# Crossbar for k, half-array scores and a new order of PSUM banks in an attention kernel with an MLP behind it

## Chip, cores, metric

One core of one Trainium2 chip. The metric is device microseconds of one execution. Each median is of executions on one chip. The experiments were run in four sets on four chips (names beginning with a, b, c, d); within a set the kernels took turns with the kernel before, whose medians were 342.99, 342.67, 342.5 and 342.35 us. Medians of different sets are thus of different chips, and differences of well under 1 us between them mean little. A run over 1.5% above the fastest of its kernel counts as slow and is left out of the ratios. Ratios are the mean time of one kernel's fast runs over that of the other's of the same rounds, so they are not quite the ratio of the medians quoted beside them.

## The reference

```python
# q, k, v: [8 batches, 8 heads, 576, 64]; x: [4608, 512]
# down: q, k, v averaged over groups of 4 rows, softmax attention over 144 rows, each result row repeated 4 times
# local: softmax attention over 576 rows, masked to |i - j| < 4
x = (out_up + out_local), heads side by side
h = x @ w_in                        # 512 -> 2048
out = gelu(h) @ w_out               # 2048 -> 512
```

## The kernel before

Names used below: PE is TensorE, DVE is VectorE, ACT is ScalarE, POOL is GpSimd, SP is the engine whose queue issues DMAs. A "crossbar" transpose is a transpose done by a DMA on its way. A transfer "lands" when its data are there. PSUM is the memory that TensorE writes, in banks; a "tag" names a buffer in it that is used over and over.

Activations stay on chip in fp16. A loop runs over nine chunks of 512 tokens. In chunk c the first product "m1" (64 matmuls of 512 columns, each four followed by a gelu on ACT) has the preparation of batch c+1 between its matmuls, and the second product "m2" (64 more) has the attention of that batch between them. `fill(n)` issues the next n of them. The parts that matter:

```python
def t_in(b, p):                     # k of one pair of heads: TensorE transposes it
    nat = nat6(ld[b % 2]["kn"])
    tr = ppool.tile([128, 1024], F16, tag="tr", name="tr_k")
    for c in range(NCK):            # 6
        nc.tensor.transpose(tr[:, CH * c:CH * c + CH], nat[:, c, 2 * p:2 * p + 2, :], I128[0:CH, 0:CH])
    for hh in range(2):             # zero-padded copy for each head
        r = slice(64 * hh, 64 * hh + 64)
        nc.vector.tensor_copy(out=kz[r, p, hh, :], in_=tr[r, 0:S])
    k_sums(p)
...
def attn(b, fill, n0, n1, n2):      # n0, n1, n2 = 6, 9, 9
    fill(n0)
    if b == 1: v_down_pe(b)         # TensorE sums v of batch 1 in groups of four
    scores(b, 0)
    fill(n1)
    mask(0)
    s_lo(b)                         # scores of the last 16 averaged keys, PSUM tag "tr"
    for p in range(NP):             # 4 pairs of heads
        if p + 1 < NP: scores(b, p + 1)
        else: fill(4)
        av(b, p)                    # value products, PSUM tag "av", then DVE normalises
        if p + 1 < NP: mask(p + 1)
        if p == 2 and b + 1 < B:
            for i in range(NP): regroup("qn", i)     # DVE
            cross(b + 1)                             # crossbar transpose of q, issued on SP
        fill(n2 if p + 1 < NP else n2 + 4)
        t_out(b, p)                 # output transposes, PSUM tag "tr"; ACT copies xd, DVE adds xT
...
# chunk c, b = c + 1 from 2 on: loads and preparation beside m1
load6(b + 1, "qn")                  # GpSimd issues all loads
v_down(b)                           # GpSimd sums v
for p in range(NP):
    q_sums(b, p)                    # GpSimd sums q; waits for q's crossbar
    f1(4 if p == 0 else 14)
    t_in(b, p)
k_lo()
run(load_nat(b + 1)); run(load_v(b + 1))
f1()
```

The softmax here doesn't subtract the row's maximum and nothing guards it: scores larger than these inputs give would overflow.

## Time and profile before

| | before |
|---|---|
| median (lowest to highest) | 342.38 us (342.2 to 342.77, 4 runs) |
| span of the profiled run | 341.7 us, clock 1.0 |
| PE busy | 97% |
| one batch, m2 start to m2 start | 35.19 us |
| of the 50 us before m2 of chunk 0, PE idle | about 8 us (41.99 of 49.76 busy) |

The lines behind this table stand in the prediction, but for the last. To read a group of lines in order of time: the first number is the start, the second the length, and PE instructions overlap in their pipeline, so the distance of starts is the cost and not the length.

### The profile page before, as it was taken

How to read it: one execution, taken by the hardware profiler on the slowest of the kernel's cores; microseconds unless marked ns; L12 is line 12 of the kernel's file. 1: busy time of each engine (PE TensorE's matmuls, PEld its weight loads, DVE VectorE, ACT ScalarE, POOL GpSimd, SP SyncE). 2: the span in 40 equal slices, each digit the busy share in tenths (PEclk: the TensorE clock that was granted, in tenths of full speed). 3: DMA queues.
4: the chain of work that ended last, by engine and by line, in shares of the span. 5: the costliest groups of instructions: out<-in, count | busy, mean ns of one | idle time of the engine just before them, and what ended most of it. 6: DMA issues, size and time to landing. Idle time of an engine off the chain costs nothing.

```text
span 341.7 us, 6605 instructions
## 1 busy us (share of the span) xinstructions
PE 330.5 (97%) x2729; PEld 185.7 (54%) x2729; DVE 176.3 (52%) x316; ACT 201.2 (59%) x369; POOL 157.0 (46%) x212
## 2 busy tenths in 40 slices
PE   8698899999999999999999999999999999999995
PEld 4574446654665456555654575457555664444444
DVE  7755954857375737663766466736764650000000
ACT  8675666646764677367736764675467656514610
POOL 8973259545926890659165916697150000000000
PEclk9999999999999999999999999999999999999999
DMA  6999999993999499849985995699610010011012
GB/s 88 153 194 205 203 86 136 185 154 75 95 177 154 68 136 131 111 91 101 173 89 118 109 169 78 126 95 152 98 65 3 31 63 31 2 61 62 2 46 77
DMA packets 109198, 35.82 MB, mean 105 GB/s; under 512 B 85744, under 2 KB 104688, under 8 KB 109168
## 3 DMA queue, kind: packets, MB, share of 16 engines
q0 software_dynamic: 89824, 22.42, 72.6%
q1 hardware_dynamic: 14304, 3.80, 8.7%
q10 hardware_dynamic: 5040, 9.18, 7.8%
q8 instruction: 21, 0.34, 0.4%
q14 instruction: 9, 0.07, 0.1%
HBM read 44.83 MB, written 9.44 MB: 159 GB/s over the span
## 4 chain that ended last, share of the span: by engine, by line
PE 89%; DVE 4%; DMA 3%; POOL 1%; ACT 1%; issue 0%; DVEq 0%; ACTq 0%
PE m_ps L260 35%; PE m_ps L236 34%; PE sc L382 5%; PE av L442 3%; DMA q_nat<-in_q_dram 3%; PE tr_o L484 2%; PE tr_k L273 2%; DVE kdz L282 1%; PE av L434 1%; PE av L436 1%; PE sc L388 1%; PE m_ps L251 1%; DVE kz L306 1%; DVE nall L452 1%; POOL k_nat L139 1%; DVE nall L457 1%
## 5 line engine op out<-in xcount | busy, mean ns | idle before, releaser
L236 PE MATMUL m_ps<-xT,w_in_sb 128*128 128x512 f16 x568 | 129.5, 379 | 2.5 <-ACT gT L239 2.1
L260 PE MATMUL m_ps<-w_out_sb,gT 128*128 128x512 f16 x560 | 130.4, 379 | 0.0
L239 ACT ACTIVATE gT<-m_ps 128x512 f16<-128x512 f32 x142 | 84.3, 597 | 43.8 <-PE m_ps L236 43.5
L236 PEld LDWEIGHTS <-w_in_sb 128*128 128x128 f16 x568 | 53.7, 97 | 63.1 <-issue 3.7
L260 PEld LDWEIGHTS <-gT 128*128 128x128 f16 x560 | 51.9, 98 | 54.7
L264 ACT COPY out_sb<-m_ps 128x512 f32<-128x512 f32 x35 | 20.6, 589 | 41.2 <-PE m_ps L260 41.2
L282 DVE TENSOR_REDUCE kdz<-kz 128x288 f16<-128x1152 f16 x28 | 37.9, 1352 | 2.0 <-ACT kz L306 1.1
L289 POOL TENSOR_TENSOR q_t<-qT 128x288 f32<-128x288 f16 x28 | 20.5, 733 | 38.5 <-DMA qT<-q_nat 31.0
L420 DVE TENSOR_TENSOR e<-e,band 128x1152 f16<-128x1152 f16 x28 | 21.5, 767 | 28.0 <-ACT e L414 28.0
L277 DVE COPY kz<-tr_k 64x576 f16<-64x576 f16 x48 | 21.8, 455 | 25.5 <-PE tr_k L273 25.1
L487 DVE TENSOR_TENSOR xT<-tr_o,xd 128x576 f16<-128x576 f16 x28 | 21.2, 756 | 23.5 <-ACT xd L486 23.5
L457 DVE TENSOR_TENSOR nall<-av,rr 128x896 f16<-128x896 f32 x29 | 31.7, 1091 | 1.0
L255 DVE COPY out_sa<-m_ps 128x256 f32<-128x256 f32 x2 | 0.8, 424 | 55.1 <-PE m_ps L251 55.1
L112 POOL DMA_DIRECT2D k_nat<-in_k_dram x36 | 27.8, 779 | 0.0
L124 POOL DMA_DIRECT2D v_win<-in_v_dram x30 | 26.6, 921 | 0.3 <-issue 0.3
L139 POOL DMA_DIRECT2D q_nat<-in_q_dram x10 | 7.9, 790 | 40.1 <-DVE q_nat L146 40.1
L382 PE MATMUL sc<-qT,kz 128*128 128x120 f16 (+1 forms) x310 | 24.6, 217 | 0.0
L412 ACT ACTIVATE e<-sc 128x684 f16<-128x684 f32 x31 | 22.8, 736 | 0.0
L382 PEld LDWEIGHTS <-kz 128*128 128x128 f16 x320 | 21.4, 97 | 1.4 <-ACT kz L306 0.2
L486 ACT COPY xd<-tr_o 128x144 f16<-128x144 f16 x28 | 7.7, 274 | 24.5 <-PE tr_o L484 21.2
L414 ACT ACTIVATE e<-sc 128x468 f16<-128x468 f32 x31 | 17.6, 567 | 0.8 <-PE sc L382 0.7
L410 ACT ACTIVATE ed<-sc 128x288 f16<-128x288 f32 x31 | 12.6, 407 | 5.8 <-PE sc L382 5.7
(176 smaller groups left out, 385.4 us busy)
## 6 DMA issues: line engine op xcount, KB each, us to landing
out_dram<-out_sb ACTq DMA_DIRECT2D x35, 256.0 KB, 4.8
v_win<-in_v_dram POOLq DMA_DIRECT2D x40, 128.0 KB, 8.1
q_nat<-in_q_dram POOLq DMA_DIRECT2D x7, 576.0 KB, 11.4
k_nat<-in_k_dram POOLq DMA_DIRECT2D x36, 96.0 KB, 4.0
v_grp<-in_v_dram POOLq DMA_DIRECT2D x6, 512.0 KB, 7.9
w_in_sb<-in_moe_w_in_dram POOLq DMA_DIRECT2D x4, 512.0 KB, 9.9
w_out_sb<-in_moe_w_out_dram POOLq DMA_DIRECT2D x4, 512.0 KB, 19.8
k_nat<-in_k_dram POOLq DMA_DIRECT2D x1, 576.0 KB, 9.1
```

Source lines behind the costliest of these rows:

```text
L112: nc.gpsimd.dma_start(out=nat6(ld[b % 2]["kn"])[:, c, :, :], in_=k[b, :, CH * c:CH * c + CH, :].rearrange("h s d -> s h d"))
L124: nc.gpsimd.dma_start(out=L["vw"][:, j, :, 0:64], in_=v[b, :, W0[j]:W0[j] + 128, :].rearrange("h s d -> s h d"))
L236: nc.tensor.matmul(out=ps, lhsT=w_in_sb[:, fc, 128 * j:128 * j + 128], rhs=xT[:, fc, 512 * c:512 * c + 512], start=(fc == 0), stop=(fc == 3))
L239: nc.scalar.activation(out=g[:, j, :], in_=ps, func=ACTF.Gelu)
L260: nc.tensor.matmul(out=ps, lhsT=g[:, j, 128 * t:128 * t + 128], rhs=w_out_sb[:, j, :], start=(j == 0), stop=(j == NJ - 1))
L277: nc.vector.tensor_copy(out=kz[r, p, hh, :], in_=tr[r, 0:S])
L282: nc.vector.tensor_reduce(out=kdz[:, p, :, :], in_=kz[:, p, :, :].rearrange("p a (g r) -> p a g r", r=4), axis=AX.X, op=ALU.add)
L382: nc.tensor.matmul(out=dst, lhsT=kz[:, p, hh, W0[j]:W0[j] + 128], rhs=q6(b)[:, :, p, Q0[j] // 6:(Q0[j] + QW[j]) // 6], start=(b > 0), stop ...
L412: nc.scalar.activation(out=e2[:, :, 0:EA], in_=sc2[:, :, 0:EA], func=ACTF.Exp, scale=0.125)
L420: nc.vector.tensor_tensor(out=e2, in0=e2, in1=band.unsqueeze(1).broadcast_to([128, 2, S]), op=ALU.mult)
L457: nc.vector.tensor_tensor(out=nall.rearrange("p j a c -> p a j c"), in0=av4[:, :, :, 0:64], in1=rr.unsqueeze(3).broadcast_to([128, 2, 7, 6 ...
L487: nc.vector.tensor_tensor(out=xT[:, p, S * b:S * b + S].rearrange("p (g r) -> p g r", r=4), in0=tr[:, 0:S].rearrange("p (g r) -> p g r", r=4),
```

## The change

The intent is to take work from TensorE: k of batches 3 to 7 is transposed by DMA through the crossbar, and a pair of heads has its scores computed on the two halves of the array, by turns, so k needs no zero padding. The two halves write different banks, so scores take four banks. The separate bank "tr" is gone; output transposes and low-key scores move into "av". Loads and sums are put in another order, and so is batch 0 (a list of words, left out).

```diff
+    def cross_k(b):
+        nc.sync.dma_start_transpose(out=kP.rearrange("p c a t -> p (c a) t"), in_=ld[b % 2]["kn"])
...
+    def k_in(p):
+        nc.vector.tensor_copy(out=kT[:, p, :].rearrange("p (c t) -> p c t", c=NCK), in_=kP[:, :, p, :])
+        k_sums(p)
...
+        if b:
+            for j in (None, 0, 1, 2, 3, 4):
+                half(0, j)          # rows 0 to 63
+                half(1, j)          # rows 64 to 127
...
     def t_out(b, p):
-        tr = ppool.tile([128, 1024], F16, tag="tr", name="tr_o")
+        tr = ppool.tile([128, 1024], F32, tag="av", name="tr_o")[:, 0:512].bitcast(F16)
...                                  # attn
-            else:
+            if p:
                 fill(4)
...
-            fill(n2 if p + 1 < NP else n2 + 4)
+            fill(8 if p + 1 < NP else 12)
...                                  # chunk, b from 2 on
                 load6(b + 1, "qn")
-            v_down(b)
+                if b > 2: run(load_nat(b + 1))
+            if b == 2: v_down(b)
             for p in range(NP):
                 q_sums(b, p)
-                f1(4 if p == 0 else 14)
-                t_in(b, p)
-            k_lo()
+                if b == 2: f1(...); t_in(b, p)
+                else: k_in(p)
+            k_lo(b)
+            if b > 2: v_down(b)
+            elif b + 1 < B: run(load_nat(b + 1))
             if b + 1 < B:
-                run(load_nat(b + 1))
+                cross_k(b + 1)
                 run(load_v(b + 1))
```

More of the change, by code (lines that the diff above doesn't have):

```diff
@@ L50 @@
     ppool = ctx.enter_context(tc.tile_pool(name="ps", bufs=1, space=bass.MemoryType.PSUM))
+    early = ExitStack()
+    spool = [early.enter_context(tc.tile_pool(name="ps0", bufs=1, space=bass.MemoryType.PSUM))]
     ctx.enter_context(tc.manual_schedule())
@@ L65 @@
     band = cpool.tile([128, S], F16, tag="band", name="band")
+    kP = cpool.tile([128, NCK, NP, CH], F16, tag="kP", name="k_turned")
     turn6 = cpool.tile([128, 3, 120], F16, tag="turn6", name="turn6")
     qd = cpool.tile([128, NP, Sd], F16, tag="qd", name="qd")
+    kT = cpool.tile([128, NP, S], F16, tag="kT", name="kT")
+    kdT = cpool.tile([128, NP, Sd], F16, tag="kdT", name="kdT")
     kz = cpool.tile([128, NP, 2, S], F16, tag="kz", name="kz")
@@ L223, in m1 @@
         if c == 0:
-            half = [mm(), mm()]
-            for fcs in ((0, 1, 2), (3,)):
-                for j in range(2):
+            part = [mm(), mm(), spool[0].tile([128, 512], F32, tag="tr", name="m_ps")]
+            for fcs in ((0, 3), (1,), (2,)):
+                for j in range(3):
                     for fc in fcs:
-                        nc.tensor.matmul(out=half[j], lhsT=w_in_sb[:, fc, 128 * j:128 * j + 128],
-                                         rhs=xT[:, fc, 0:512], start=(fc == 0), stop=(fc == 3))
-                        if fc == 3:
-                            nc.scalar.activation(out=g[:, j, :], in_=half[j], func=ACTF.Gelu)
+                        nc.tensor.matmul(out=part[j], lhsT=w_in_sb[:, fc, 128 * j:128 * j + 128],
+                                         rhs=xT[:, fc, 0:512], start=(fc == 0), stop=(fc == 2))
+                        if fc == 2:
+                            nc.scalar.activation(out=g[:, j, :], in_=part[j], func=ACTF.Gelu)
                         yield
-        for j in range(2 if c == 0 else 0, NJ):
+        for j in range(3 if c == 0 else 0, NJ):
             ps = mm()
@@ L262, in m2 @@
                 if j == NJ - 1:
-                    osb = wpool.tile([128, 512], F32, tag="osb", bufs=5, name="out_sb")
+                    osb = wpool.tile([128, 512], F32, tag="osb", bufs=4, name="out_sb")
                     nc.scalar.copy(out=osb, in_=ps)
@@ L270, in t_in @@
         nat = nat6(ld[b % 2]["kn"])
-        tr = ppool.tile([128, 1024], F16, tag="tr", name="tr_k")
+        if p % 2:
+            trf = ppool.tile([128, 1024], F32, tag="av", name="tr_k")
+        else:
+            trf = spool[0].tile([128, 2048], F32, tag="sc", name="tr_k")
+        tr = trf[:, 0:512].bitcast(F16)
         for c in range(NCK):
@@ L274, in t_in @@
                                 I128[0:CH, 0:CH])
-        for hh in range(2):
-            r = slice(64 * hh, 64 * hh + 64)
-            nc.vector.tensor_copy(out=kz[r, p, hh, :], in_=tr[r, 0:S])
+        nc.vector.tensor_copy(out=kT[:, p, :], in_=tr[:, 0:S])
+        k_sums(p)
+    def k_in(p):
+        nc.vector.tensor_copy(out=kT[:, p, :].rearrange("p (c t) -> p c t", c=NCK), in_=kP[:, :, p, :])
         k_sums(p)
@@ L281, in k_sums @@
         with nc.allow_low_precision(reason="sums of four, kept in fp16 as before"):
-            nc.vector.tensor_reduce(out=kdz[:, p, :, :], in_=kz[:, p, :, :].rearrange("p a (g r) -> p a g r", r=4),
+            nc.vector.tensor_reduce(out=kdT[:, p, :], in_=kT[:, p, :].rearrange("p (g r) -> p g r", r=4),
                                     axis=AX.X, op=ALU.add)
@@ L313, in q_from, with v_down_mm @@
         cp(out=q6(b)[:, :, p, :], in_=tr.rearrange("p (r t) -> p r t", r=6))
-    def v_down_mm(L, va):
-        for j in range(5):
+    def v_down_mm(L, va, js=range(5)):
+        for j in js:
             n = 112 if j < 4 else 128
@@ L319, in v_down_mm @@
                              start=(j == 0), stop=(j == 4))
-        nc.tensor.matmul(out=va[1], lhsT=GL.rearrange("p a c -> p (a c)"), rhs=L["vw"][:, 4, :, 0:64],
-                         start=True, stop=True)
+            if j == 4:
+                nc.tensor.matmul(out=va[1], lhsT=GL.rearrange("p a c -> p (a c)"), rhs=L["vw"][:, 4, :, 0:64],
+                                 start=True, stop=True)
     def v_down_d(L, va, cp):
@@ L336, in v_down_pe, with k_lo @@
         v_down_m(L, va)
-    def k_lo():
+    def k_lo(b):
         KLb = KL.rearrange("p (a c) -> p a c", c=160)
@@ L341, in k_lo @@
             r = slice(64 * hh, 64 * hh + 64)
-            nc.vector.tensor_copy(out=KLb[r, :, 16 * hh:16 * hh + 16], in_=kdz[r, :, hh, 128:Sd])
+            nc.vector.tensor_copy(out=KLb[r, :, 16 * hh:16 * hh + 16], in_=kdT[r, :, 128:Sd] if b else kdz[r, :, hh, 128:Sd])
     def v_down(b):
@@ L358, in s_lo @@
     def s_lo(b):
-        s_lo_mm(ppool.tile([128, 512], F32, tag="tr", name="sl"))
+        s_lo_mm(ppool.tile([128, 1024], F32, tag="av", name="sl"))
         s_lo_exp(b)
@@ L374, in scores @@
     def scores(b, p):
-        sc = ppool.tile([128, 1536], F32, tag="sc", name="sc")
-        scores_mm(b, p, sc[:, 0:1024], sc[:, 1024:1536])
+        sc = spool[0].tile([128, 2048], F32, tag="sc", name="sc")
+        scores_mm(b, p, sc[:, 0:1024], sc[:, 1024:2048])
         for i in range(3):
@@ L380, in scores_mm, with q_win, padded, half @@
     def scores_mm(b, p, sA, sC):
-        def local(dst, hh, j):
-            nc.tensor.matmul(out=dst, lhsT=kz[:, p, hh, W0[j]:W0[j] + 128],
-                             rhs=q6(b)[:, :, p, Q0[j] // 6:(Q0[j] + QW[j]) // 6], start=(b > 0),
-                             stop=(b > 0 or j in (2, 4)))
-        for hh in range(2):
+        def q_win(r, j):
+            return q6(b)[r, :, p, Q0[j] // 6:(Q0[j] + QW[j]) // 6]
+        def padded(dst, hh, j):
+            nc.tensor.matmul(out=dst, lhsT=kz[:, p, hh, W0[j]:W0[j] + 128], rhs=q_win(slice(0, 128), j),
+                             start=False, stop=(j in (2, 4)))
+        def half(hh, j):
+            r = slice(64 * hh, 64 * hh + 64)
+            o = 512 * hh
+            if j is None:
+                nc.tensor.matmul(out=sA[:, o + EA:o + EA + Sd], lhsT=kdT[r, p, 0:128], rhs=qd[r, p, :],
+                                 start=True, stop=True)
+                return
+            dst = sA if j < 3 else sC
+            o += Q0[j] - (0 if j < 3 else EA)
+            nc.tensor.matmul(out=dst[:, o:o + QW[j]], lhsT=kT[r, p, W0[j]:W0[j] + 128], rhs=q_win(r, j),
+                             start=True, stop=True)
+        if b:
+            for j in (None, 0, 1, 2, 3, 4):
+                half(0, j)
+                half(1, j)
+        for hh in range(0 if b else 2):
             o = 512 * hh
@@ L389, in scores_mm @@
                              start=True, stop=True)
-            if b == 0:
-                nc.tensor.matmul(out=sA[:, o:o + EA], lhsT=I128, rhs=nb[:, 0:EA], start=True, stop=False)
+            nc.tensor.matmul(out=sA[:, o:o + EA], lhsT=I128, rhs=nb[:, 0:EA], start=True, stop=False)
             for j in range(3):
-                local(sA[:, o + Q0[j]:o + Q0[j] + QW[j]], hh, j)
-        for hh in range(2):
+                padded(sA[:, o + Q0[j]:o + Q0[j] + QW[j]], hh, j)
+        for hh in range(0 if b else 2):
             o = EC * hh - EA
-            if b == 0:
-                nc.tensor.matmul(out=sC[:, o + EA:o + S], lhsT=I128, rhs=nb[:, EA:S], start=True, stop=False)
+            nc.tensor.matmul(out=sC[:, o + EA:o + S], lhsT=I128, rhs=nb[:, EA:S], start=True, stop=False)
             for j in range(3, 5):
-                local(sC[:, o + Q0[j]:o + Q0[j] + QW[j]], hh, j)
+                padded(sC[:, o + Q0[j]:o + Q0[j] + QW[j]], hh, j)
         e = e_t[p % 3] if b else e_t0[p]
@@ L414, in exps @@
             nc.scalar.activation(out=e2[:, :, EA:S],
-                                 in_=sC[:, 0:2 * EC].rearrange("p (a c) -> p a c", c=EC),
+                                 in_=(sC.rearrange("p (a c) -> p a c", c=512)[:, :, 0:EC] if sC.shape[1] > 512
+                                      else sC[:, 0:2 * EC].rearrange("p (a c) -> p a c", c=EC)),
                                  func=ACTF.Exp, scale=0.125)
@@ L497, in to_exp, with attn @@
         nc.scalar.activation(out=dum[:, 1:2], in_=dum[:, 0:1], func=ACTF.Exp)
-    def attn(b, fill, n0, n1, n2):
+    def attn(b, fill, n0, n1):
         fill(n0)
@@ L533, in spin @@
     def spin(n):
-        ps = ppool.tile([128, 512], F32, tag="tr", name="spin")
+        ps = spool[0].tile([128, 512], F32, tag="tr", name="spin")
         for _ in range(n):
@@ L540 @@
     PLAN0 = """
-        BAND Rk0:D Rq0:D Tk0:mm0 Rk1:D Tq0:mm1 KZ10:A NB Rq1:D Tk1:av QD0:A KD10:D QT0:A KZ11:D KD00:A
-        spin1 Tq1:mm1 KZ00:A KD01:D QD1:A Rk3:D spin1 S0:sc KZ01:A Rk2:D QT1:D KD11:A Rq2:D Tk2:mm0 E20
-        Rq3:D KD12:A Tq3:av KD02:A KZ12:A Tq2:mm1 QD3:D QT3:D KZ02:A QD2:D E00 QT2:D spin2 S1:av+mm0 E10
-        Tk3:mm1 E11 S2:sc KD13:D E01 KZ13:D E21 KD03:D E22 spin1 VD:av KL E02 KZ03:D E12 SL:mm0 VLM
-        VDe:A S3:sc EL AV0:av E23 AV2:mm0+mm1 E13 NA0 E03 gelu spin3 AV1:sc NA2 TO0:av XT0:A NA1 spin2
-        AV3:mm0+mm1 TO2:av NA3 XT2:A TO1:sc XT1:A spin3 TO3:av M1A:mm0+mm1 XT3:A M1B
+        BAND Rk0:D Rq0:D Tk0:mm0 Rk1:D Tq0:mm1 KD10:A NB KD00:A Tk1:av KZ10:A QT0:D KZ00:A KZ11:D QD0:D
+        KD01:A Rq1:D KD11:A spin5 S0:sc KZ01:D Tq1:mm0 Rk3:D E00 Rk2:D E10 Tk3:mm1 QD1:D QT1:D Tk2:av
+        E20 KZ13:D S1:sc KD02:A KD12:A Rq3:D KZ12:A KZ03:D Tq3:mm0 E01 Rq2:D E21 QT3:D E11 QD3:D KD13:D
+        spin4 Tq2:mm0 KD03:D KZ02:A S3:sc QD2:D KL QT2:A VD0:av E23 SL:mm1 VD1 E03 VD2 E13 VD3 VD4 S2:sc
+        VDe:A VLM EL AV0:av E22 AV3:mm0+mm1 E02 NA0 E12 spin3 AV1:sc gelu NA3 TO0:av XT0:A NA1 spin2
+        TO3:mm0+mm1 AV2:av XT3:A NA2 TO1:sc M1X:mm0+mm1+tr XT1:D TO2:av M1Y XT2:A M1B
     """
@@ L561, in banks @@
         if sl == "sc":
-            t = ppool.tile([128, 1536], F32, tag="sc", name="sc")
+            t = spool[0].tile([128, 1536], F32, tag="sc", name="sc")
             return [t[:, 0:512], t[:, 512:1024], t[:, 1024:1536]], t[:, 0:1024]
@@ L591 @@
         elif nm[:2] == "M1":
-            f1_0(6 if nm == "M1A" else 2)
+            f1_0(6 if nm == "M1X" else 3)
         elif nm[0] == "R":
@@ L605 @@
         elif nm == "KL":
-            k_lo()
+            k_lo(0)
         elif nm == "SL":
@@ L610 @@
             s_lo_exp(0)
-        elif nm == "VD":
-            slot["VD"] = banks(arg)[0]
-            v_down_mm(L0, slot["VD"])
+        elif nm[:2] == "VD" and nm != "VDe":
+            if p == 0:
+                slot["VD"] = banks(arg)[0]
+            v_down_mm(L0, slot["VD"], (p,))
         elif nm == "VDe":
@@ L631 @@
         elif nm[:2] == "XT":
-            cp(out=xT[:, p, 0:S], in_=slot["o", p][1][:, 0:S])
+            half, two = slot["o", p]
+            if two is not None:
+                cp(out=xT[:, p, 0:S], in_=two[:, 0:S])
+            else:
+                cp(out=xT[:, p, 0:512], in_=half[0])
+                cp(out=xT[:, p, 512:S], in_=half[1][:, 0:S - 512])
     load6(1, "kn")
@@ L645, in home @@
             def home(i):
-                tag, n = (("tr", 512), ("av", 1024), ("sc", 1536))[i % 3]
-                return ppool.tile([128, n], F32, tag=tag, name=f"t_{tag}")[:, 0:512]
+                tag, n = (("av", 1024), ("sc", 1536), ("tr", 512))[i % 3]
+                return (ppool if tag == "av" else spool[0]).tile([128, n], F32, tag=tag, name=f"t_{tag}")[:, 0:512]
             regroup("kn", 0)
@@ L653 @@
                 tr, _ = t_reg("kn", p, home(p), False)
-                kz_from(p, 0, tr, nc.vector.tensor_copy)
-                kz_from(p, 1, tr, nc.scalar.copy)
+                nc.vector.tensor_copy(out=kT[:, p, :].rearrange("p (t r) -> p t r", r=6),
+                                      in_=tr.rearrange("p (r t) -> p t r", r=6))
                 if p + 2 < NP:
@@ L665 @@
                 if p == 0:
-                    k_lo()
-                f1(5)
+                    k_lo(b)
+                f1(4)
             load6(2, "qn")
@@ L673 @@
                 load6(b + 1, "qn")
-            v_down(b)
+                if b > 2:
+                    run(load_nat(b + 1))
+            if b == 2:
+                v_down(b)
             for p in range(NP):
                 q_sums(b, p)
-                f1(4 if p == 0 else 14)
-                t_in(b, p)
-            k_lo()
+                if b == 2:
+                    f1(4 if p == 0 else 14)
+                    t_in(b, p)
+                else:
+                    k_in(p)
+            k_lo(b)
+            if b > 2:
+                v_down(b)
+            elif b + 1 < B:
+                run(load_nat(b + 1))
             if b + 1 < B:
-                run(load_nat(b + 1))
+                cross_k(b + 1)
                 run(load_v(b + 1))
         f1()
+        if c == 0:
+            early.close()
+            spool[0] = ctx.enter_context(tc.tile_pool(name="ps1", bufs=1, space=bass.MemoryType.PSUM))
         f2 = filler(m2(c))
@@ L686 @@
             to_exp()
-            attn(b, f2, 6, 9, 8 if b == 1 else 9)
+            attn(b, f2, 6, 9)
         f2()
```

## The prediction

> **What bounds the kernel now.** I read the page first (busy shares, the chain that ended last), then the table by stretches, then the order of time within one batch. The page says TensorE:
>
> ```profile
> PE 330.5 (97%) x2729; PEld 185.7 (54%) x2729; DVE 176.3 (52%) x316; ACT 201.2 (59%) x369; POOL 157.0 (46%) x212
> PE 89%; DVE 4%; DMA 3%; POOL 1%; ACT 1%; issue 0%; DVEq 0%; ACTq 0%
> ```
>
> The kernel loops over nine chunks of 512 tokens. In chunk c, "m1" is 64 matmuls of 512 columns (L236) with the next batch's preparation between them, "m2" is 64 more (L260) with that batch's attention between them. Starts of L236 in the chain that ended last, one per chunk, show a period of 141.98 - 106.79 = 35.19 us:
>
> ```profile
> 106.79 0.86 PE m_ps L236 x4
> 107.91 3.02 PE m_ps L236 x14
> 111.19 3.02 PE m_ps L236 x14
> ...
> 141.98 0.86 PE m_ps L236 x4
> ```
>
> A block of 14 takes 3.02 us (0.216 each), yet the next starts 3.28 us later: the six transposes of k between them cost 0.26 us. The rest of a batch, from the order of time on PE around 97 us (start, duration), is read from start to start:
>
> ```profile
> 97.10 0.20 PE L480 MATMUL tr_o<-Iw,nall 66*128 66x66 f16 x1
> ...
> 97.46 0.23 PE L388 MATMUL sc<-qd,kdz 128*128 128x144 f16 x1
> ...
> 98.12 0.19 PE L434 MATMUL av<-v_d,ed 128*128 128x65 f16 x1
> ...
> 98.66 2.11 PE L260 MATMUL m_ps<-w_out_sb,gT 128*128 128x512 f16 x9
> ```
>
> So the output transposes take 0.36 us, the twelve scores 0.66 (55 ns each), the value products 0.54. A batch's work is 128 x 0.2157 + 4 x (0.26 + 0.66 + 0.54 + 0.35) + 0.25 for the low keys = 35.1 of the 35.19: a batch has almost no waiting on PE. Waiting is only before 50 us. There 19.0 us hold 16.48 of PE, then it is full:
>
> ```profile
> 31.00:50.00 19.00, 16.48 (x113) 8.40 (x112) 12.59 (x20) 11.37 (x21) 6.61 (x10) 1.00 1.34 164
> 50.00:71.60 21.60, 21.60 (x223) 13.33 (x222) 12.81 (x21) 13.04 (x26) 16.77 (x21) 1.00 1.62 157
> ```
>
> The columns are stretch, length, busy PE, PEld, DVE, ACT, POOL, clock, DMA share, GB/s. Work removed from PE shortens a batch only as far as nothing else starts to bind.
>
> **What the Trainium skill says.** (1) "TensorEngine Tiling (Array Packing)", section Key Properties: different tiles can load and multiply in parallel, but changing the tiling mode drains TensorE. Nothing here runs in a half-array mode, so the trace before can neither confirm it nor size the drain. (2) Same page, Gotcha 1: row tiles must write different PSUM banks. That is why scores now take four banks and the former "tr" bank is gone. (3) "TensorE: Matmul & The Clock Gate", Part 3, The mechanism: weights load beside running matmuls of another row group. The 65-column products already run at 0.31 us for ten with their weight loads, so weights are not a bound at 31 ns. (4) "DMA: Bandwidth & Descriptors", Issuing engines are not separate DMA queues: all queues share the 16 DMA engines. The trace agrees in part: q's crossbar transpose took 6.2 us to land where no q load ran beside it (242.8 us), 9.2 to 14.2 elsewhere.
>
> **The change part by part.**
>
> Transposes of k. Batches 3 to 7 lose four groups: 5 x 4 x 0.26 = **-5.2 us** on PE. In exchange SP issues one more crossbar transpose per batch, with some 30 us of slack before its reader, and DVE does a copy from SBUF and a sum over half as many elements (the sum takes 1.35 us now). None of that is on the path.
>
> Scores. Six pairs in place of twelve singles: 6 x 55 ns = 0.33 us if a pair runs in the time of one, plus a drain on entry and on return. The trace gives a ceiling for a drain: a 65-column product is shown 194 ns long at a pitch of 31, so some 0.16 us of pipeline. I choose 0.1 each, an estimate: 0.53 against 0.66, so 28 x 0.13 = **-3.6 us** for batches 1 to 7.
>
> Start. The new order of batch 0 puts exponentials of pair 0 before the late loads of pairs 2 and 3, replaces spins by nine m1 products, and batch 1 needs no zero-padded halves: DVE's copy of 0.75 serves both heads, ACT's 0.63 copy goes and the sum halves. m1 of chunk 0 then no longer waits (19.0 - 16.5 = 2.5 us); I expect m2 of chunk 0 some 4 to 5 us before its 49.8. But PE then needs v of batch 1 for its group sums:
>
> ```profile
> 37.47 1.02 POOL L155 DMA_DIRECT2D v_win<-in_v_dram  x1 [1.17 <-DMA w_out_sb<-in_moe_w_out_dram]
> 51.05 1.26 PE L318 MATMUL va<-v_win,Gb 112*128 112x512 f16 x5
> ```
>
> That last load took 12.4 us to land, at 49.9; DMA is saturated until then and the change moves no bytes out. The sums now end at 52.38; they can end at 50.4 at best: **-2.0 us**, however well the start is packed.
>
> The lost "tr" bank. The output transposes and the low-key scores now live in "av". So the value products of pair p+1 cannot start before DVE has added xT of pair p. This is where I expect the gain to go. DVE around pair 2:
>
> ```profile
> 99.12 0.24 DVE L456 RECIPROCAL rr<-av 128x14 f32<-128x14 f32 x1
> 99.39 1.09 DVE L457 TENSOR_TENSOR nall<-av,rr 128x896 f16<-128x896 f32 x1
> 100.40 0.75 DVE L420 TENSOR_TENSOR e<-e,band 128x1152 f16<-128x1152 f16 x1
> 101.06 1.16 DVE L146 COPY q_nat<-q_nat 96x768 f16<-96x768 f16 x4
> 102.14 0.75 DVE L487 TENSOR_TENSOR xT<-tr_o,xd 128x576 f16<-128x576 f16 x1
> ```
>
> In program order the four regroupings of q stand before xT of pair 2. From the reciprocal to the end of xT is 3.77 us; with 0.2 from the end of the products to the reciprocal and 0.06 for the release that is 4.03. PE has between the products of pairs 2 and 3 eight m2 products, the output transposes and four more: 1.73 + 0.35 + 0.86 = 2.94. So PE waits 1.1 us, in batches 1 to 6 (batch 7 regroups nothing): **+6.6 us**. Between pairs 0, 1 and 2 there is no regrouping: products end, then 2.07 to the end of the transposes, 0.2 + 0.28 + 0.03 + 0.76 + 0.06 for xd and xT = 3.40, against 2.94 + 0.53 of scores on PE = 3.47: just hidden. Faster scores would only turn into a wait there.
>
> The end of a batch. m2's products between are now 63 of 64 before the last transposes' end, against 59. From 105.54 (end of transposes) xT of pair 3 needs until 106.81, 1.27 us. PE has one m2 product and three of m1 that don't need pair 3: 0.86. It waits 0.45 us in seven batches: **+3.2 us**. Low keys in "av": the first products wait for their exponential, about 0.05 x 7 = **+0.35 us**.
>
> Sum: -5.2 - 3.6 - 2.0 + 6.6 + 3.2 + 0.35 = -0.65, so 341.7 us.
>
> **The rivals.**
>
> Rival 1: the new waits stay hidden, and PE's saving is the time: 342.3 - 5.2 - 3.6 - 2.0 = 331.5. For it: the m2 products were redistributed (four more before the products of pairs 1 and 2), plainly to cover the bank. Against it: at pair 3 the four were there before, and the regrouping still stands ahead of xT. Half of this, or drains near zero, gives about 336.
>
> Rival 2: the drain is the whole 0.16, the scores gain nothing: 345. For: the skill's page names a drain, twice per pair of heads, 56 times. Against: only the ceiling is in the trace.
>
> Rival 3: DMA. GpSimd's sums of v move behind those of q, which wait for q's crossbar. From m1's start I have: landing at 5 to 6.2, q sums 4.8, v sums 5.4, done at 16.4; the value products need them at 18.8. Some 2.4 us of slack; k's loads now run beside the crossbar, and if it lands 4 us later PE loses 1.6 us in five batches: 350. Against: the loads follow one another in one queue, and q's own load is already beside it. Also, PE waiting from 46 to 50 us for v could lower its clock for a while; the clock row shows no such dip now.
>
> **Range and chances.** I give the sum 65 in 100, the faster half-way (336) 25 and the slower side (346) 10: 0.65 x 341.7 + 0.25 x 336 + 0.10 x 346 = 340.7 us. The range that holds 8 in 10 is 335 to 345. Two per cent is 6.85 us: faster needs under 335.5, which takes both waits mostly hidden: 0.18. Slower needs over 349.2, DMA lateness in every batch: 0.03. Within: 0.79.
>
> **What would show it.** Right: L236 blocks without gaps in chunks 2 to 6; scores of a pair at 0.45 to 0.6 us from first to next instruction; PE idle about 1.1 us before the first value product of pair 3, released by DVE's xT, in batches 1 to 6 and not in 7; 0.45 us before the fourth product of each m1; the sums of v of batch 1 waiting for v_win. PE's busy share should fall below 97% while the time hardly moves. Wrong: no idle at pair 3 (then 331 to 336), scores at 0.65 or more (345), or value products of pair 0 waiting for v_d or v_lm of GpSimd (over 346).

## The result, and the profile after

The changed kernel takes **352.88 us** (350.65 to 354.83, 4 runs) against 342.38; the ratio is 1.0303, with a 95% interval of 1.0233 to 1.0373. It is slower by 3%, outside the predicted range. A second set of two runs gave 350.78 and 353.14.

The page of the profiled run (350.65 us, span 348.9) shows what "less work" means here. PE's busy time fell by 3.3 us while the span grew by 7.2:

```profile
PE 327.2 (94%) x2610; PEld 171.7 (49%) x2610; DVE 145.5 (42%) x292; ACT 198.7 (57%) x364; POOL 156.5 (45%) x212
PEclk9999989999999998999999999999999999999999
...
PE 69%; DMA 8%; POOL 8%; DVE 7%; issue 6%; ACT 1%; POOLq 0%
```

PE's share of the chain that ended last fell from 89% to 69%; DMA rose from 3% to 8%, GpSimd ("POOL") from 1% to 8%. The clock row (40 slices of 8.72 us) has two dips that the kernel before has not, at 44 to 52 and 131 to 140 us. The starts of m1 and m2, read from the order of time on PE, say where. "Again" is the second profile of the changed kernel (span 349.1).

| us | before | after | again |
|---|---|---|---|
| m1 of chunk 0 starts | 30.55 | 26.59 | 27.03 |
| m2 of chunk 0 starts | 49.76 | 43.65 | 44.09 |
| m1 of chunk 1 starts | 71.43 | 71.18 | 73.11 |
| m2 chunk 1 to m2 chunk 2 | 35.19 | 35.21 | 35.21 |
| m2 chunk 2 to m2 chunk 3 (attention of batch 3) | 35.20 | **42.09** | **40.23** |
| m2 chunk 3 to m2 chunk 4 | 35.19 | 35.22 | 35.23 |
| m2 of chunk 7 to the end | 45.2 | 44.8 | 44.9 |

The 6 us that the new start wins are gone again before chunk 1. All steady batches are as long as before to 0.1 us. One batch is 5 to 7 us longer. The waits of PE after, longest in total first (engine and line, what ended the wait, us in total, times, longest):

```profile
PE av L470 <- DVE xT L523: 5.8, 7, 0.9
PE av L470 <- POOL v_d L367: 3.3, 1, 3.3
PE va L335 <- DMA v_win<-in_v_dram: 2.9, 4, 1.1
PE m_ps L247 <- DVE xT L523: 2.1, 7, 0.3
PE av L472 <- POOL v_lm L371: 1.7, 1, 1.7
```

The first and fourth are the two waits that the prediction worked out: 0.92 us before the value products of pair 3 in six batches (the seventh entry is short), 0.29 in the fourth product of m1 in seven. Both in order of time in one batch (lines between left out):

```profile
179.08 1.03 PE L271 MATMUL m_ps<-w_out_sb,gT 128*128 128x512 f16 x4
181.02 0.19 PE L470 MATMUL av<-v_d,ed 128*128 128x65 f16 x1 [0.92 <-DVE xT L523]
...
184.73 0.81 PE L247 MATMUL m_ps<-xT,w_in_sb 128*128 128x512 f16 x3
185.84 1.46 PE L247 MATMUL m_ps<-xT,w_in_sb 128*128 128x512 f16 x6 [0.29 <-DVE xT L523]
```

The idle time in brackets begins when the pipeline is empty. What a wait costs is again read from start to start. Four products at 0.2157 us lead from 179.08 to 179.94, and the next instruction starts at 181.02: the wait costs 1.08 us. Three lead from 184.73 to 185.38, and the fourth starts at 185.84: 0.46 us.

The second and fifth waits are batch 3. In order of time on PE, then on GpSimd:

```profile
125.89 0.24 PE L411 MATMUL sc<-qd,kdT 64*128 64x144 f16 x2
125.96 0.43 PE L416 MATMUL sc<-qT,kT 64*128 64x120 f16 x10
129.66 0.19 PE L470 MATMUL av<-v_d,ed 128*128 128x65 f16 x1 [3.27 <-POOL v_d L367]
131.57 0.21 PE L472 MATMUL av<-v_lm,eL 128*128 128x65 f16 x1 [1.72 <-POOL v_lm L371]
```

```profile
120.87 0.73 POOL L306 TENSOR_TENSOR q_t<-qT 128x288 f32<-128x288 f16 x1 [11.55 <-DMA qT<-q_nat]
...
128.35 1.27 POOL L367 TENSOR_TENSOR v_d<-v_t 128x512 f16<-128x512 f32 x1
```

GpSimd waited 11.55 us for q's crossbar, then summed q, then v, and the value products were waiting for v. The two waits are 5.0 of the 6.9 us. Another 1.2 are the eight m2 products behind them: they took 2.94 us from start to start (132.48 to 135.42) where 1.73 is usual, at a granted clock of 0.63 from 132 to 136 us. The crossbar transposes on SP's queue, start and time to issue, show what q's was behind:

```profile
91.32 6.70 SPq L162 DMA_TRANSPOSE k_turned<-k_nat  x1
103.14 7.73 SPq L159 DMA_TRANSPOSE qT<-q_nat  x1
125.23 2.93 SPq L162 DMA_TRANSPOSE k_turned<-k_nat  x1
145.22 3.58 SPq L159 DMA_TRANSPOSE qT<-q_nat  x1
```

The DMA view of the stretches around the first two gives the time from issue to landing:

```profile
k_turned<-k_nat SPq DMA_TRANSPOSE x1, 15.0
...
qT<-q_nat SPq DMA_TRANSPOSE x1, 17.7
```

k of batch 3 is the only one whose load was left behind the sums of q (those of batch 2), so its crossbar is issued among v's loads and needs 15.0 us, until 106.3. q's is issued at 103.1 and needs 17.7. In the later batches k's crossbar runs before v's loads and takes 4.8 to 4.9 us, and q's of batch 4 takes 11.3.

The start: PE on its group sums of v of batch 1, and the table by stretches (columns as in the prediction) after:

```profile
47.12 0.38 PE L335 MATMUL va<-v_win,Gb 112*128 112x512 f16 x1 [0.57 <-DMA v_win<-in_v_dram]
48.06 0.38 PE L335 MATMUL va<-v_win,Gb 112*128 112x512 f16 x1 [0.56 <-DMA v_win<-in_v_dram]
49.54 0.55 PE L335 MATMUL va<-v_win,Gb 128*128 128x512 f16 x1 [1.10 <-DMA v_win<-in_v_dram]
...
51.16 3.02 PE L271 MATMUL m_ps<-w_out_sb,gT 128*128 128x512 f16 x9
```

```profile
44.00:48.00 4.00, 2.25 (x9) 0.60 (x7) 0.00 (x0) 1.93 (x3) 3.92 (x6) 1.00 2.07 132
48.00:52.00 4.00, 2.84 (x18) 1.02 (x18) 0.69 (x1) 1.27 (x3) 3.52 (x6) 0.70 1.66 181
```

PE came early and waited for the loads as predicted. Then the granted clock fell to 0.70 of full, and the nine m2 products, shown 2.10 us long at full clock, took 3.02.

### The profile page after: what moved, and what is told of

It reads as the page before. It is cut to its first block, busy times and chain, and to the rows that moved or that the text cites. A ratio compares the mean times of both kernels' runs of the same rounds, so it can differ in the third digit from the quotient of the medians.

```text
span 348.9 us, 6372 instructions
## 1 busy us (share of the span) xinstructions
PE 327.2 (94%) x2610; PEld 171.7 (49%) x2610; DVE 145.5 (42%) x292; ACT 198.7 (57%) x364; POOL 156.5 (45%) x212
## 4 chain that ended last, share of the span: by engine, by line
PE 69%; DMA 8%; POOL 8%; DVE 7%; issue 6%; ACT 1%; POOLq 0%
PE m_ps L271 29%; PE m_ps L247 27%; DMA w_out_sb<-in_moe_w_out_dram 5%; DMA v_win<-in_v_dram 4%; DVE xT L523 3%; PE av L478 3%; PE sc L416 2%; DVE q_nat L154 2%; PE tr_o L520 2%; PE av L470 2%; POOL v_win L166 1%; PE sc L411 1%; DVE e L456 1%; PE av L472 1%; PE m_ps L262 1%
## 5 line engine op out<-in xcount | busy, mean ns | idle before, releaser
L271 PE MATMUL m_ps<-w_out_sb,gT 128*128 128x512 f16 x560 | 135.0, 384 | 0.0
L247 PE MATMUL m_ps<-xT,w_in_sb 128*128 128x512 f16 x564 | 126.4, 379 | 2.3 <-DVE xT L523 2.1
L493 DVE TENSOR_TENSOR nall<-av,rr 128x896 f16<-128x896 f32 x30 | 32.7, 1091 | 1.0
L447 ACT ACTIVATE e<-sc 128x684 f16<-128x684 f32 x32 | 23.5, 735 | 0.0
L299 DVE TENSOR_REDUCE kdT<-kT 128x144 f16<-128x576 f16 x28 | 21.0, 750 | 0.8
L492 DVE RECIPROCAL rr<-av 128x14 f32<-128x14 f32 x30 | 7.4, 246 | 30.9 <-PE av L478 30.9
L470 PE MATMUL av<-v_d,ed 128*128 128x65 f16 x120 | 11.6, 195 | 9.2 <-DVE xT L523 5.8
L472 PEld LDWEIGHTS <-eL 128*128 128x128 f16 x128 | 9.1, 98 | 13.0 <-issue 11.3
```

Source lines behind the costliest of these rows:

```text
L247: nc.tensor.matmul(out=ps, lhsT=w_in_sb[:, fc, 128 * j:128 * j + 128], rhs=xT[:, fc, 512 * c:512 * c + 512], start=(fc == 0), stop=(fc == 3))
L271: nc.tensor.matmul(out=ps, lhsT=g[:, j, 128 * t:128 * t + 128], rhs=w_out_sb[:, j, :], start=(j == 0), stop=(j == NJ - 1))
L299: nc.vector.tensor_reduce(out=kdT[:, p, :], in_=kT[:, p, :].rearrange("p (g r) -> p g r", r=4), axis=AX.X, op=ALU.add)
L447: nc.scalar.activation(out=e2[:, :, 0:EA], in_=sc2[:, :, 0:EA], func=ACTF.Exp, scale=0.125)
L493: nc.vector.tensor_tensor(out=nall.rearrange("p j a c -> p a j c"), in0=av4[:, :, :, 0:64], in1=rr.unsqueeze(3).broadcast_to([128, 2, 7, 6 ...
```

## The experiments

There were fifteen runs. Theory A: batch 3 is long because v's sums stand behind a late q crossbar. Theory D: q's crossbar is late because k's, started beside v's loads, is in front of it. Rivals: B, q itself is what is missing; C, the loads of k beside q's crossbar slow it. Theory E is the wait for the "av" bank, F the slow clock.

### Sums of v first

```diff
-            if b == 2: v_down(b)
+            if b > 1: v_down(b)
...
-            if b > 2: v_down(b)
-            elif b + 1 < B: run(load_nat(b + 1))
+            if b == 2: run(load_nat(b + 1))
```

> The changed kernel with one edit: GpSimd sums v of batches 3 to 7 before it waits for q's crossbar, as the kernel before did, instead of after the sums of q. Theory A (the 6.9 us by which batch 3 is longer come from the sums of v queued behind a late q crossbar): the waits of the value products for v_d and v_lm (5.0 us in the profile, plus some slow clock after) disappear, batch 3 is back at 35 to 36 us, the time falls by 5 to 8 us to 344 to 348. Rival B (q itself, 13 us late, is what the scores wait for): batch 3 stays at 41 us or more and the time within 2 us of 352.9.

Measured: 344.98 us (344.67 to 346.37). The waits for v_d and v_lm are gone, and batch 3 takes 35.20 us although q's crossbar still landed 17.1 us after issue. Theory A holds. Rival B falls for this kernel; where a batch comes sooner, q itself does become the wait (see "the crossbar alone" and "nine m2 products").

### Loads of the next k after the sums

```diff
                 load6(b + 1, "qn")
-                if b > 2: run(load_nat(b + 1))
...
             if b > 2: v_down(b)
-            elif b + 1 < B: run(load_nat(b + 1))
+            if b + 1 < B: run(load_nat(b + 1))
```

> The changed kernel with one edit: for batches 3 to 6 the loads of the next k are issued after the sums of q and v, not at the head of the chunk beside q's crossbar. Theory C (the early k loads slow q's crossbar): it lands within 10 us of issue, the stall in batch 3 is gone, 345 to 348 us. Rival D (k's crossbar, held up by v's loads, runs into q's crossbar on the same queue): now every batch issues k's crossbar beside v's loads, so q's crossbar lands 13 us or more after issue in several batches and the time is 353 or more, up to 375.

Measured: 389.98 us, the largest effect of the study and more than the 375 expected at most. Batch 4's two crossbars, time to landing:

```profile
k_turned<-k_nat SPq DMA_TRANSPOSE x1, 15.2
...
qT<-q_nat SPq DMA_TRANSPOSE x1, 19.4
```

Batches 3 to 6 all do now what only batch 3 did: k's crossbars take 15.0 to 16.3 us and q's 17.2 to 20.7, and batches take 42 to 48 us. Rival C falls in batch 3: k's crossbar stands there as before, only the k loads beside q's crossbar are gone, and q's still takes 17.2 us (17.7 with them). Rival D of the expectation is theory D, and it holds: the late k crossbar, put into every batch, makes q's late in batches 3 to 6.

### k by TensorE again

The crossbar part undone: `t_in` for every batch from 2 on, loads and sums in the old order; half-array scores, banks and start stay.

> The changed kernel without its crossbar part: k of batches 2 to 7 is transposed by TensorE and loads and sums stand in the order of the kernel before; half-array scores, four banks, new start stay. If the crossbar is the cause of the loss in batch 3: no such stall, but 5 x 1.04 us of transposes come back while the waits for the av bank stay: steady batches of 36.2 us, 352.9 - 7 + 5 = about 350, with runs alike to 1 us. If the loss has another cause: batch 3 stays above 40 us and the time is 357 or so.

Measured: 349.62 us (349.23 to 349.97). No wait in batch 3, batches of 36.25 us: 35.22 plus the 1.04 of the transposes. The rest of the change costs a batch about what the crossbar saves it.

### The crossbar alone

The kernel before, with `cross_k`, k loads at the head of the chunk from batch 3 on, and `k_in` copying into the zero-padded halves.

> The kernel before with the crossbar part alone (k of batches 3 to 7 by crossbar, loads of k at the head of the chunk, sums of v before sums of q; zero-padded scores, old banks, old start). If removing the transposes is worth its PE time where no new bank wait takes it: 342.4 - 5.2 = 337 (336 to 339). If crossbar traffic costs as much as it saves: 341 or more, with q's crossbar landing above 13 us in batch 3.

Measured: 339.33 and 342.03 us in two runs, 347.48 and 348.39 in two that count as slow. Steady batches take 34.28 us. The profile is of a slow run: there the first scores of batch 3 waited 8.2 us for q's sums, with q's crossbar landing 20.9 us after issue. So the loss comes with the crossbar and does not need the rest of the change. Its size seems to change from run to run; the two fast runs, which have no profile, lie 1.9 and 4.6 us above the median of "the crossbar alone, with k of batch 3 early" below (another chip).

### k of batch 3 early

```diff
                 load6(b + 1, "qn")
-                if b > 2: run(load_nat(b + 1))
+                run(load_nat(b + 1))
...
             if b > 2: v_down(b)
-            elif b + 1 < B: run(load_nat(b + 1))
```

> The changed kernel with one edit: k of batch 3 is loaded at the head of its chunk, as k of batches 4 to 7 is, and not behind the sums of q; the late sums of v stay. Theory D (batch 3 stalls because its k crossbar, issued when v's loads begin, lands after 15 us and holds back q's crossbar on the same queue): k's crossbar lands in 5 to 8 us, q's within 12, no wait for v_d in batch 3, 345 to 346 us. Rival C (the loads of k beside q's crossbar are the cause): batch 3 stalls as before, and batch 2 too, 352 or more.

Measured: 343.32 us (341.95 to 344.75). Batch 3 takes 35.22 us with v's sums still late. k's crossbar for batch 3 is issued at 84.3 instead of 91.3 and landed after 9.7 us, q's after 11.0:

```profile
84.33 3.04 SPq L162 DMA_TRANSPOSE k_turned<-k_nat  x1
104.14 3.57 SPq L159 DMA_TRANSPOSE qT<-q_nat  x1
```

k's crossbar ends 10 us before q's is issued, and q's issue takes 3.57 us instead of 7.73. Theory D holds, up to an open end given below. One misplaced load of k was worth 9.6 of the 10.5 us by the medians, and with it moved the kernel lies inside the predicted range. In the profiles batch 3 alone is 6.9 us shorter.

### The crossbar alone, with k of batch 3 early

The kernel of "the crossbar alone" with the edit above.

> The kernel before with the crossbar part alone and k of batch 3 loaded at the head of its chunk. Theory D: no run has the 10 us wait of batch 3 that two of four runs of the crossbar alone had; 342.5 - 5 x 0.92 = 338 us in every run. Rival: the wait comes back in some runs.

Measured: **337.42 us** (337.26 to 337.71, four runs), ratio 0.9853 (0.9819 to 0.9887). That is 5.1 us less by the medians, near the predicted -5.2 us for the transposes, and no slow run. In the profile five batches are 0.92 us shorter each, 4.6 in all; m2 of chunk 0 also starts 0.83 us sooner, for which nothing here gives a cause.

### Nine m2 products before pair 3's value products

The kernel with the sums of v first, and:

```diff
             if p:
-                fill(4)
+                fill(9 if p == 3 else 4)
...
-            fill(8 if p + 1 < NP else 12)
+            fill(8 if p + 1 < NP else 7)
```

> The kernel with the sums of v first (345.0 us) and one more edit: of the m2 products of a batch, nine instead of four stand before the value products of pair 3, and seven instead of twelve behind them. Theory E (the regrouping of q ahead of xT makes the value products of pair 3 wait 0.9 us for the av bank in batches 1 to 6): the wait goes, at most 0.1 us returns behind, 5 us less: 340 us. Rival: the wait moves on to the output transposes of pair 3 or to the end of the batch: 343 to 345.

Measured: 341.41 and 342.46 us, and 346.64 and 346.71 in two that count as slow. PE's waits for xT before the value products are gone from the table, and steady batches take 34.27 us against 35.22. Theory E holds at 0.95 us a batch: of the 1.08 us of the wait, 0.13 come back before the output transposes of pair 3. In return the scores of batch 3, sooner at their place, waited 3.3 us for the late q in the profile (the 342.46 us run), and that batch took 39.2 us: the late crossbar takes back what comes early.

### Group sums of v of batch 1 later

The kernel with the sums of v first; `v_down_pe(1)` moved from before `scores(b, 0)` to behind `fill(n1)` and `mask(0)`.

> The kernel with the sums of v first and one more edit: TensorE's group sums of v of batch 1 stand behind the scores of pair 0 and nine m2 products instead of before them. Theory F (idling between 45 and 51 us for v's loads also slows the clock): 2.5 us of work fills the wait, the clock stays nearer to 1, the time falls by 2 to 3.5 us to 342. Rival: only the work moves and the clock drops all the same: 344.

Measured: 344.23 us (342.86 to 345.08), 0.75 less by the medians, which are of two chips. m1 of chunk 1 starts at 69.14 instead of 73.34 and the clock stays at 1.00 between 44 and 56 us, but 2.6 us of waits for q's sums and a batch 3 of 38.05 us came back. Inconclusive by the time; the start behaves as theory F says.

### Idle products during the wait

The kernel with k of batch 3 early; three products of zeros into a free "sc" tile before each of the five group sums.

> The kernel with k of batch 3 early (343.3 us) and one more edit: three idle products stand before each of the five group sums of v of batch 1, so TensorE works through its wait for v's loads. Theory F (the slow clock after that wait, 0.50 and 0.65 of full between 48 and 56 us, is TensorE's idling): the clock stays at 0.95 or more, the nine m2 products after it run at 0.22 us each, and the time falls by 1 to 2 us to 341.5 to 342.3. Rival: the clock falls all the same and the time stays.

Measured: 342.94 us (342.25 to 344.12). The table by stretches of this kernel:

```profile
44.00:48.00 4.00, 4.00 (x21) 1.78 (x19) 0.00 (x0) 2.08 (x3) 3.92 (x7) 1.00 2.01 128
48.00:52.00 4.00, 3.29 (x25) 1.36 (x24) 0.22 (x1) 0.84 (x3) 3.75 (x5) 1.00 1.53 174
52.00:56.00 4.00, 4.00 (x48) 2.34 (x47) 2.21 (x4) 3.10 (x8) 2.89 (x4) 1.00 2.17 167
```

The clock is 1.00 throughout (mean 0.999 or more in every run; 0.990 to 0.995 in three of four without), against 0.50 and 0.65 in the two stretches from 48 to 56 us without the idle products. So the cause of the slow clock is shown. Its price is less clear. From the start of the last group sum to the low-key scores it takes 2.92 us (50.53 to 53.45) against 5.28 (49.74 to 55.02), but v's last load came 0.8 us later, and m1 of chunk 1 starts 1.2 us sooner. The medians differ by only 0.4 us, on two chips and with ranges that overlap: no gain in time is shown.

### Heads in order

The kernel with the sums of v first; all six scores of head 0, then all six of head 1.

> The kernel with the sums of v first and one more edit: the six scores of head 0 all stand before the six of head 1, so no neighbours lie on different halves of the array except once. If the halves run side by side only in turns: a pair's scores take 0.75 us instead of 0.53 and 28 x 0.2 = 5.6 us come on top, less what waits take up: 348 to 351. If the gain comes from half the rows alone, the time stays at 345.

Measured: 347.16 us (346.91 to 348.58), batches of 35.73 us, 0.51 longer. From the first score to the next instruction it takes 0.57 us against 0.44 by turns, and 0.66 with zero padding on the full array. So taking turns is worth 0.13 us a pair, less than the 0.2 expected. Half rows alone give nothing: entering them costs 0.09 us here too (in one batch the six m2 products before them make way at 159.35, and the scores start at 159.45), and 0.57 + 0.09 is the 0.66 of the full array.

### All mends together

k of batch 3 early, sums of v first, nine m2 products, group sums late.

> The changed kernel with four edits together: k of batch 3 loaded at the head of its chunk, sums of v before those of q, nine m2 products before the value products of pair 3, group sums of v of batch 1 behind nine m2 products. Each removed its wait alone; together the steady batch should be 34.27 us against 35.19 before, batch 3 too, and the start 2 us ahead of the kernel before: 342.5 - 6 x 0.92 - 2 = 335 us (333 to 337), 0.978 of the kernel before, alike in all runs. If the mends collide (q's crossbar earlier beside v's loads): a stall in one batch and 338 to 343.

Measured: 338.16 us (335.36 to 340.32, six runs), ratio 0.9863 (0.9815 to 0.991). The profile, of the best run, has batches of 34.27 us and batch 3 as well. The expected 335 us came in two runs; the median missed it by 3. The runs spread over 5 us, with a mean clock of 1.0 in the fastest and 0.989 in the slowest.

### The changed kernel and the mended kernel again

> The changed kernel itself once more, for a second profile: its four runs lay between 350.7 and 354.8 us. If the spread is that of the late q crossbar in batch 3: batch 3 again takes 41 to 46 us, all other batches 35.2, and the difference to the first profile lies in batch 3 and in the start.

350.78 and 353.14 us; the profile is the column "again" above. Against the kernel before, batch 3 is 5.0 us longer and the start 1.7; no other batch of the table, nor the end, differs by more than 0.3 us.

> The mended kernel once more, for a second profile. If this one is among the slow ones (above 337 us): either the clock row shows a stretch under 1 near 50 us, or some batch shows a wait for qd or v_d; the first theory expects the former, with batches of 34.27 us all along.

341.13 and 339.2 us, both at a clock of 0.99. The stretches of the mended kernel in this run show why. (PE's wait for the last v loads of batch 1 ends at 50.6 us here.)

```profile
48.00:52.00 4.00, 1.08 (x4) 0.29 (x3) 0.16 (x1) 0.59 (x1) 3.19 (x5) 0.92 1.64 167
52.00:56.00 4.00, 3.41 (x37) 2.31 (x37) 1.42 (x3) 2.27 (x5) 2.64 (x4) 0.50 2.17 165
56.00:60.00 4.00, 4.00 (x30) 1.88 (x29) 1.88 (x3) 1.16 (x4) 2.41 (x3) 0.73 1.84 194
```

Half clock after 52 us, m1 of chunk 1 3.7 us later than in the fast profile (71.36 against 67.62; v's last load was itself 1.2 us later), and a batch 6 of 36.6 us. In that batch PE waited 2.1 us for DVE: its four copies of q took 3.46 us from 239.11 on, where 1.16 is usual. Beside them, until 242.3, ran GpSimd's sums of v, which had waited 5.9 us for a load. That the sums slowed the copies is not tested.

### The mended kernel kept busy

Mended, with the group sums back before the scores and the idle products in the wait.

> The mended kernel with the group sums of v of batch 1 back before the scores and three idle products ahead of each of the five. If the spread of the mended kernel is the slow clock: clock 0.998 or more in every run and all runs within 1.5 us of each other, 342.9 - 6 x 0.95 = 337 us. If it is late transfers: runs spread by 3 us or more at full clock.

Measured: 337.83 us (336.46 to 338.95), clock 1.000 in all four runs. The spread falls from 5 to 2.5 us. The group sums were moved back at the same time; still, on this chip the mended kernel ran at a clock of 0.99 and took 339.2 and 341.13 us, so the clock was probably part of it. What is left is at full clock, so it is something else; the kernel before, too, spread from 342.03 to 346.06 us in this set. The expectation asked for 1.5 us or for 3, and the answer lies between.

> As d1, but the sums of v of batches 3 to 7 stay behind those of q, as the change has them; k's crossbar then lands in 4.8 us, before v's loads begin. If the order of the sums matters only where q is late: 337 us like d1. If it keeps transfers apart: 1 us less and a smaller spread than d1; if late sums still cost: 339 or more.

Measured: 337.74 to 340.03 us in five runs, and one of 860.51 us, which nothing explains and no other run repeats; it is left out as slow. Late sums win nothing: in the profile they cost one wait of 1.9 us for v_lm.

## Why the prediction was wrong

Step by step, in the order of its sum:

- **Transposes, -5.2 us.** Right: TensorE's transposes put back cost 1.04 us a batch, and the crossbar alone with k of batch 3 early is 5.1 us faster by the medians, 4.6 of it in the five batches of its profile.
- **Scores, 0.53 us a pair.** Right: 0.44 from the first score to the next instruction plus 0.09 on entering, 0.53 in all. (After, the distance from the five output transposes to the scores is 0.35 us; it was 0.26.) The 0.09 is measured only as a longer distance on entry; a drain on leaving can't be told from the rest.
- **Pair 3's wait, 1.1 us a batch.** Right in place, cause and size: 1.08 from start to start (the view's 0.92 leaves out the pipeline's tail); removing it gave 0.95.
- **End of a batch, 0.45 us.** Right in place, cause and size: 0.46 from start to start. (The numbers shown, 1.27 - 0.86, make 0.41; the release, 0.06 elsewhere in the text, is not written there.) It is the one wait left in the mended kernel.
- **A steady batch as a whole** was to take 35.19 - 1.04 - 0.52 + 1.1 + 0.45 + 0.05 = 35.23 us; it takes 35.22, and the measured parts add up to the same. Half-array scores and their bank changes bring a batch nothing net: 34.27 us mended against 34.28 with the crossbar alone.
- **Start, -2.0 us.** The "at best" was right for the group sums; what follows was wrong. m2 of chunk 0 starts 6.1 us sooner (4 to 5 were expected) and the scores behind the group sums start at 50.45 against 52.38, 1.9 us sooner (1.2 in the other profile, where v's last load landed later; 0.3 in the kernel with the sums of v first). But the prediction mentioned that waiting could lower the clock and then gave it no time. From there to the low-key scores it takes 3.57 us (50.45 to 54.02) against 2.60 before, though the scores should have gained 0.13: the slow clock costs 1.1 us (2.1 in the other profile). With pair 3's wait of batch 1, counted above, m1 of chunk 1 starts 0.25 us sooner in one profile and 1.68 later in the other.
- **"with some 30 us of slack before its reader ... None of that is on the path".** This is the step that failed most, +5.0 to +6.9 us. The slack of k was there. What it left out is that k's crossbar stands on the queue on which q's has only 2.4 us of slack, and that for batch 3 alone the load of k was left behind the sums of q, so its crossbar meets v's loads. q's crossbar then took 17.7 us to land (11.3 in the next batch), and PE waited 5.0 us for v's sums behind it. The diff shows that exception (`elif b + 1 < B`), and I read it only as a special case of batch 2. The chance of a slower kernel (0.03) was tied to lateness in every batch; one batch was enough.
- **Rival 3** named the wait that came, value products waiting for v's sums, but expected it of k's loads and in five batches or none. Its sum of slack was good: q's crossbar landed 13.4 us after m1's start, 7.2 later than its 6.2; less 2.4 of slack that is 4.8, and PE waited 5.0. (In batches 4 to 6 it landed 7.0 to 8.2 us after, inside the slack.) Experiment "loads of the next k after the sums" shows those loads are better where they are. Two readings of the trace before are slightly off: its landings lie 4.9 to 6.6 us after m1's start in batches 3 to 6 (not 5 to 6.2), and the last crossbar is issued at 243.12 us (not 242.8).

With the two misses put in, the sum is -0.65 + 6.9 for batch 3 + 1.1 for the clock = 7.35 us; the profiled run has 7.2.

What stays open: q's crossbar was late with k's before it on the queue and with v's last loads beside both. Moving k's load takes k's crossbar away from both, so the share of each isn't told apart. The runs of 353 to 355 us were never profiled. The spread of 2.5 us at full clock in the mended kernel isn't explained.

## What to carry to other kernels

When work moves from an engine to a DMA queue, the question is not only when its reader needs it but what stands behind it on that queue, and what else is in flight when it starts: work the order out for the first batch too, where the loop differs. Here the matrix engine came early to a load, gained nothing by it and lost its clock for some microseconds. And before a bank is given up, list what its reuse now waits for; five matmuls moved in between were enough to hide it here.

## What the Trainium skill lacked or had wrong

- "TensorE: Matmul & The Clock Gate", HAM oscillation, gives as its rule no idle gaps over about 3.4 us, and under A second HAM failure mode says that frequent short idling can cost the clock too, without an amount. Here no single wait between the five group sums was over 1.1 us in the changed kernel; PE was busy 2.25 of 4 us, and the granted clock fell to 0.70 in the next 4 us (0.50 in the kernel with k of batch 3 early). With idle products in the waits it stayed at 1.00. With the group sums of v later, 1.00 busy of 4 us (48 to 52 us, after 3.96 of the 4 before) kept it at 1.00; in the mended kernel 1.08 of the same 4 us, after 4.00, was followed by 0.50. So busy time in such a stretch doesn't decide, and the limit isn't pinned down. Half clock as the low state (What's actually happening) agrees.
- "TensorEngine Tiling (Array Packing)", Key Properties: the drain on a change of mode has no size there. Entering the half-array mode lengthened the distance by 0.09 us. Two row tiles by turns took 0.44 us for twelve scores against 0.66 on the full array, 1.5 times (1.25 with the entry), where the page's table under Theoretical Speedup says up to 2.
- "DMA: Bandwidth & Descriptors": nothing on what a crossbar transpose costs beside other traffic. The same 0.6 MB took 4.8 us with nothing else in flight and 8.4 to 16.4 beside v's loads of many small packets, and one issued before another had landed took 12.4 to 21.0.
